# Seven products for eight in the first layer's last 1024 tokens, and second-layer weights in half-row portions

## Chip, cores, metric

One Trainium2 chip, one core. The metric is the device time of one execution in microseconds (us); lower is better.

## What is computed

Sliding-window attention, then two feed-forward layers on the same 2304 tokens, all in float32:

```python
scores = scale * np.matmul(q, k.transpose(0, 1, 3, 2))      # 4 x 8 heads x 576 x 64
scores = np.where((rel >= 0) & (rel < 64), scores, -1e9)
attn = softmax(scores); x = attn @ v                        # x: 2304 x 512
h = x @ w_in1;  g = np.maximum(h, 0.0) ** 2;  x = g @ w_out1    # 512 -> 2048 -> 512
h = x @ w_in2;  g = np.where(h > 0, h, np.exp(np.minimum(h, 0)) - 1);  out = g @ w_out2
```

The four weight matrices come as 64-bit floats and are turned into 32-bit values on the chip ("decode").

## The kernel before

The 2304 tokens are five blocks, `BLOCKS = [512, 256, 512, 512, 512]`, t = 0 to 4. The first layer's 2048 middle features are 16 groups of 128, j = 0 to 15. Every float32 operand is kept as a pair, a rounded high part and the rest as a low part (`split`, L105: ScalarE copies the high part, L107, and VectorE subtracts, L108), and every product is three matmuls: high by high, high by low, low by high (`mm3`, L355).

The first layer walks over (t, j), L735. `m_h(t, j)`, L362, is the first product of one group: 12 matmuls into a bank `ph`, then on ScalarE relu (L376) and square (L377) into `g`, then the split into `gs`, of which there are three. `m_out(t, j)`, L381, is the second product: 12 matmuls that add `gs` times the group's output weights to four banks `o`. First products run two groups ahead (LA = 2). After group 15 the block's result goes to DRAM (`x2d`). While block t is worked on, the attention of block t + 1 is done by pairs of heads p = 0 to 3 (a "unit"): `u_S` (scores, softmax: L276 on TensorE, L284 and L305 on VectorE, L289 on ScalarE), `u_T` (transposes, L317), `u_PV` (L330), `u_X` (split of the result into `xs`).

In block 0 the weights of the first layer are decoded (`w_split`, L152, with `decode64`, L135: one absolute value on ScalarE, then clamp, shift, and two merges on VectorE), each unit of `UNITS` one output group and the input group two further on.

The second layer's weights are prepared meanwhile. `make(i, p)`, L172, takes rows p and p + 8 of one matrix, decodes each row as a whole, forms the seven combinations that seven products need, splits each and writes it as a 256 KB piece (`wo`, L190) to DRAM. There are 16 such calls, at the places in `MAKE`, L433: two in block 1, four each in blocks 2 and 3, six in block 4. Their pieces pass through the four tiles `pt`, in block 4 through tiles of `xs`.

The second layer uses seven products of halves for eight already, in both products, on three stretches of 768 tokens (`step`, L596, `prod`, L564, `prod2`, L683). `x_make`, L506, forms the seven token operands, `unit_load`, L486, brings the prepared weights. Its order is written out by hand, by `in_turn`, L557, and a list.

The order on each engine inside the first layer is set by a scheduler that follows the program's order as a priority; the instructions of an engine then run in that order, each waiting for its semaphores. All loads and writes here are issued on one queue (SyncE, SP).

Of the kernel before, what the change touches and what calls it, by code (L numbers as in the profile page):

```python
# [25 lines left out]
def window_attention_then_two_mlps(  # L26
# [13 lines left out]
    nc = tc.nc  # L40
    HP, _, NT = k.shape
# [42 lines left out]
    def zeros():  # L84
        for x in qd:
            zero_q(x, nc.vector)
# [16 lines left out]
    last = {}  # L103

    def split(hi, lo, x, eng):  # L105

        last["hi"] = nc.scalar.activation(out=hi, in_=x, func=AF.Copy)  # L107
        last["lo"] = eng.tensor_tensor(out=lo, in0=x, in1=hi.bitcast(F32), op=ALU.subtract)  # L108

    def copy(out, in_, eng):  # L110
        if eng is nc.scalar:
            nc.scalar.activation(out=out, in_=in_, func=AF.Copy)
        else:
            eng.tensor_copy(out, in_)
# [8 lines left out]
    UNITS = [[(j, 0)] for j in range(LA)]  # L123
    UNITS += [[(j, 1)] + ([(j + LA, 0)] if j + LA < NJ else []) for j in range(NJ)]
    NU = len(UNITS)

    def w_load(u):

        m = len(UNITS[u])
        r = wts.tile([P, m, KD * P, 2], U32, tag=f"w{u}", name="wraw")  # L130
        for k, (j, i) in enumerate(UNITS[u]):
            nc.sync.dma_start(out=r[:, k].rearrange("p f w -> p (f w)"), in_=(w_in1, w_out1)[i][j])
        raw_w[u] = r

    def decode64(y, yf, lower, upper):  # L135

        nc.scalar.activation(out=yf, in_=upper.bitcast(F32), func=AF.Abs)  # L137
        nc.vector.tensor_scalar(  # L138
            out=yf, in0=yf, scalar1=SHORT, scalar2=TALL, op0=ALU.max, op1=ALU.min
        )  # L140
        nc.vector.tensor_scalar(
# [3 lines left out]
        nc.vector.scalar_tensor_tensor(  # L145
            out=y, in0=upper, scalar=0xC0000000, in1=y, op0=ALU.bitwise_and, op1=ALU.bitwise_or
        )
        nc.vector.scalar_tensor_tensor(
# [3 lines left out]
    def w_split(u):  # L152
# [5 lines left out]
        w = wts.tile([P, m, 2, KD * P], F32R, tag=f"w{u}", name="w")  # L158
        split(w[:, :, 0, :], w[:, :, 1, :], yf, nc.vector)
# [9 lines left out]
    wd1 = [drp.tile([P, 7, 2, HW], F32, name=f"wd1_{p}") for p in range(NP)]  # L169
    wd2 = {n: drp.tile([P, NP, 2, HW], F32, name=f"wd2_{n}") for n in ORD2}  # L170

    def make(i, p, big, small):  # L172

        y = big([P, 2, KD * P], "y")
        w = big([P, KD * P, 2], "praw")
        for r, j in enumerate((p, p + NP)):
            nc.sync.dma_start(out=w.rearrange("p f w -> p (f w)"), in_=(w_in2, w_out2)[i][j])
            decode64(y[:, r], y[:, r].bitcast(F32), w[:, :, 0], w[:, :, 1])
        y = y.bitcast(F32)
        q11, q12, q21, q22 = y[:, 0, :HW], y[:, 0, HW:], y[:, 1, :HW], y[:, 1, HW:]  # L180

        def put(k, x):
            o = small([P, 2, HW], "wo")
            if i:
                z = o.rearrange("p y (m a j) -> p y a m j", m=FT, j=TB)
                split(z[:, 0], z[:, 1], x.rearrange("p (a m j) -> p a m j", m=FT, j=TB), nc.vector)
            else:
                split(o[:, 0], o[:, 1], x, nc.vector)
            d = wd2[k][:, p] if i else wd1[p][:, ORD1.index(k)]
            nc.sync.dma_start(out=d, in_=o.bitcast(F32))  # L190

        def sub(x, a, b, op=ALU.subtract):
            nc.vector.tensor_tensor(out=x, in0=a, in1=b, op=op)

        if i:
            put(1, q11)
            put(2, q21)
            put(3, q22)
            sub(q12, q12, q11)
            put(5, q12)  # L200
            sub(q22, q22, q12)
            put(6, q22)
            sub(q11, q22, q11)
            put(7, q11)
            sub(q21, q21, q22)
            put(4, q21)
        else:
            put("a11", q11)
            put("a12", q12)
            put("a22", q22)  # L210
            sub(q21, q21, q22, ALU.add)
            put("s1", q21)
            sub(q11, q21, q11)
            put("s2", q11)
            sub(q12, q12, q11)
            put("s4", q12)
            sub(q22, q22, q11)
            put("s3", q22)

    raw = {}  # L220
# [3 lines left out]
    def u_load(u, parts="qkv"):  # L224
# [18 lines left out]
        if "k" in parts:  # L243
# [6 lines left out]
            if e:  # L250
                nc.vector.memset(kr[:, 0:WIN], 0.0)
# [14 lines left out]
    def u_S(u, alloc):  # L266
# [5 lines left out]
        for b0, m in banks(t):  # L272
# [9 lines left out]
            for i in range(m):  # L282
                c, b = slice(i * P, (i + 1) * P), b0 + i
                nc.vector.tensor_tensor_reduce(  # L284
# [4 lines left out]
                last["act"] = nc.scalar.activation(  # L289
# [4 lines left out]
            nc.vector.tensor_scalar(  # L294
                out=r, in0=sm[:, b0:b0 + m], scalar1=1.0e-9, scalar2=None, op0=ALU.add
            )
            nc.vector.reciprocal(out=r, in_=r)
            for i in range(m):
                c, b = slice(i * P, (i + 1) * P), b0 + i
                if t == 1:  # L300
                    nc.scalar.activation(
                        out=pb[:, c], in_=pb[:, c], func=AF.Copy, scale=rc[:, b:b + 1]
                    )
                    continue
                last["dve"] = nc.vector.tensor_scalar(  # L305
# [4 lines left out]
    def u_T(u, alloc):  # L310

        pts = []
        for b0, m in banks(u[0]):
# [5 lines left out]
            copy(pt[:, :m * P], ps[:, :m * P], nc.scalar)  # L319
# [16 lines left out]
    def u_X(u, ps):  # L336
        t, p = u
        n = BLOCKS[t]
        s = xs[t, p] = xp.tile([P, 2, NMAX], F32R, tag=f"xs{p}", name="xs")
        split(s[:, 0, :n], s[:, 1, :n], ps[:, :n], nc.vector)  # L340
# [21 lines left out]
    def m_h(t, j):  # L362
# [13 lines left out]
        nc.scalar.activation(out=g[:, :n], in_=ps[:, :n], func=AF.Relu)  # L376
        nc.scalar.activation(out=g[:, :n], in_=g[:, :n], func=AF.Square)  # L377
        split(s[:, 0, :n], s[:, 1, :n], g[:, :n], nc.vector)
        gs[t, j] = s

    def m_out(t, j):  # L381
# [12 lines left out]
        if j == NJ - 1:  # L394
            for m, ps in enumerate(acc[0]):
                e = e_tile(t)
                copy(e[:, :n], ps[:, :n], nc.vector if m % 2 else nc.scalar)
                nc.sync.dma_start(out=x2d[t][:, m, :], in_=e[:, :n])
# [33 lines left out]
    its = [(t, j) for t in range(NB) for j in range(NJ)]  # L432
    MAKE = {(1, 2), (1, 9)} | {(t, j) for t in (2, 3) for j in (1, 5, 9, 13)} | {(4, j) for j in (0, 1, 3, 4, 6, 7)}  # L433
    makes = [(i, p) for i in range(2) for p in range(NP)]
# [4 lines left out]
    CH = KD // 2  # L439
    la = []  # L440

    def e_tile(t):
        if la:
            return la[0].tile([P, 512], F32, tag="e4", name="ev", bufs=4)
        return at.tile([P, 512], F32, tag="pt", name="ev", bufs=4)

    turn = [0, 0]
    spare = []

    def big(shape, name):  # L450
        if name == "y" and la:
            turn[0] += 1
        if not la or turn[0] % 2:
            return wts.tile(shape, U32, tag="y", name=name, bufs=2)
        return wts.tile(shape, U32, tag="w0" if name == "y" else "w1", name=name)

    def small(shape, name):
        if la:
            if not spare:
                for k in range(KD):  # L460
                    x = xp.tile([P, 2, 2, HW], F32R, tag=f"xs{k}", name=name)
                    spare.extend((x[:, 0], x[:, 1]))
            turn[1] += 1
            return spare[turn[0] % 2 * KD + turn[1] % KD]
        return at.tile(shape, F32R, tag="pt", name=name, bufs=4)
# [3 lines left out]
    def gs_tile(name, n, m):  # L469
        k = g_turn[0] = (g_turn[0] + 1) % m  # L470
        if k < 4:
            return la[0].tile([P, 2, n], F32R, tag=f"gs{k}", name=name, bufs=1)
        return wts.tile([P, 2, n], F32R, tag=f"w{LA + NJ - 1}" if k == 4 else f"w{NJ - 1}", name=name)

    RING = [f"w{k}" for k in range(7, 15)]
# [30 lines left out]
    def x_make(b):  # L506
# [12 lines left out]
        b11, b12, b21, b22 = q[0, 0], q[0, 1], q[1, 0], q[1, 1]  # L519

        def put(i, x):
            if i < 5:
                o = wts.tile([P, 2, CH, NH], F32R, tag=f"w{LA + i}", name="xo")
            else:
                o = la[0].tile([P, 2, CH, NH], F32R, tag=f"xo{i}", name="xo", bufs=1)
            X[b, i] = o
            split(o[:, 0], o[:, 1], x, nc.vector)

        def sub(x, a, b):
            nc.vector.tensor_tensor(out=x, in0=a, in1=b, op=ALU.subtract)  # L530
# [3 lines left out]
        yield  # L534
        sub(b12, b12, b11)
# [28 lines left out]
    def prod(b, p, i, ps, first, final):  # L564
# [9 lines left out]

    tmp = {}
    rot2 = [0]

    def elu(h, x):
# [3 lines left out]
        nc.scalar.activation(out=r, in_=x, func=AF.Relu, scale=-1.0)  # L582
        last["act"] = nc.scalar.activation(out=r, in_=r, func=AF.Exp, scale=-1.0)
        last["dve"] = nc.vector.scalar_tensor_tensor(
# [5 lines left out]
    def add(out, a, b):  # L590
        nc.vector.tensor_tensor(out=out, in0=a, in1=b, op=ALU.add)  # L591

    def sub(out, a, b):
        nc.vector.tensor_tensor(out=out, in0=a, in1=b, op=ALU.subtract)

    def step(b, p, i):  # L596
# [4 lines left out]
        if i in (1, 6, 7):  # L601
            prod(b, p, i, q["x"], i == 1, False)
            nc.scalar.activation(out=tmp[i], in_=q["x"][:, :NH], func=AF.Copy)  # L603
# [27 lines left out]
    def g_split(b, k, p):  # L631
        if (b, k) == (NSB - 1, 4):
            if p % 2 == 0:
                room[0] = wts.tile([P, 2, 2, NH], F32R, tag=f"w{LA + p // 2}", name="g4")
# [4 lines left out]
        split(s[:, 0], s[:, 1], g[SRC[k]], nc.vector)  # L639
# [10 lines left out]
    def store(b, k, y, lo, hi, ms):  # L650
# [8 lines left out]
        for m in ms:  # L659
# [5 lines left out]
            nc.vector.transpose(out=o[:, :, m], in_=x.rearrange("p (b i) -> p b i", i=TB))  # L665
# [3 lines left out]
        def leave():  # L669
            for a in range(AB):  # L670
                c0 = dh * HW + a * FT * TB
                q_ = nc.scalar if n < NH and a % 2 else nc.sync
# [10 lines left out]
    def prod2(b, k, p, lo=0, hi=NH, ms=range(FT)):  # L683
# [20 lines left out]
        if k in (1, 6, 7):  # L704
            for m in range(FT):
                nc.scalar.activation(out=tmp[-k][:, m], in_=x[m][:, :NH], func=AF.Copy)
# [26 lines left out]
    for i in range(LA):  # L733
        m_h(*its[i])
    for i, (t, j) in enumerate(its):  # L735
# [146 lines left out]
```

## Time and profile before

| | |
|---|---|
| median of 3 runs | 840.34 us (840.02 to 842.02) |
| the profiled execution | 840.35 us, of which span 838.6 us |
| TensorE busy | 824.0 us |
| VectorE busy | 607.2 us |
| ScalarE busy | 546.3 us |
| moved by DMA | 185.48 MB |

The span runs from the first to the last instruction. Busy time is the time in which at least one instruction of the engine runs; TensorE's matmuls are pipelined and their ends modelled.

### The profile page before, as it was taken

How to read it: one execution, taken by the hardware profiler on the slowest of the kernel's cores; microseconds unless marked ns; L12 is line 12 of the kernel's file. 1: busy time of each engine (PE TensorE's matmuls, PEld its weight loads, DVE VectorE, ACT ScalarE, POOL GpSimd, SP SyncE). 2: the span in 40 equal slices, each digit the busy share in tenths (PEclk: the TensorE clock that was granted, in tenths of full speed). 3: DMA queues.
4: the chain of work that ended last, by engine and by line, in shares of the span. 5: the costliest groups of instructions: out<-in, count | busy, mean ns of one | idle time of the engine just before them, and what ended most of it. 6: DMA issues, size and time to landing. Idle time of an engine off the chain costs nothing.

```text
span 838.6 us, 14237 instructions
## 1 busy us (share of the span) xinstructions
PE 824.0 (98%) x4956; PEld 752.6 (90%) x4956; DVE 607.2 (72%) x1511; ACT 546.3 (65%) x1262; POOL 5.6 (1%) x21
## 2 busy tenths in 40 slices
PE   6899999999999999999999999999999999999998
PEld 5687879998888888888888899999999999999998
DVE  7999987675428575386696756698676799566875
ACT  6787867686447566575576667666477766477652
POOL 2000000000000000000000000000000000000000
PEclk9999999999999999999999999999999999999999
DMA  9991226455236563343869987878977876877832
GB/s 308 376 395 32 55 75 216 140 187 184 78 92 203 194 218 105 126 152 138 290 238 348 358 294 279 294 263 280 301 266 262 321 259 216 281 268 272 303 123 57
DMA packets 92807, 185.48 MB, mean 221 GB/s; under 512 B 43840, under 2 KB 50496, under 8 KB 84288
## 3 DMA queue, kind: packets, MB, share of 16 engines
q1 hardware_dynamic: 91904, 184.38, 64.6%
q8 instruction: 39, 0.64, 0.3%
q10 hardware_dynamic: 832, 0.20, 0.1%
q14 instruction: 32, 0.26, 0.1%
HBM read 145.75 MB, written 38.80 MB: 220 GB/s over the span
## 4 chain that ended last, share of the span: by engine, by line
PE 96%; DMA 1%; DVE 1%; ACT 1%; SPq 0%; issue 0%
PE ph L358 24%; PE o L358 24%; PE po L696 20%; PE px L569 8%; PE po L569 6%; PE py L569 6%; PE pa L276 3%; PE pa L330 2%; PE pa L317 2%; DMA wr<-wd 1%; PE px L696 1%; DVE pb L284 1%; DVE pb L305 1%; DMA qd<-in_q_dram 0%; PE po L276 0%; ACT pb L289 0%
## 5 line engine op out<-in xcount | busy, mean ns | idle before, releaser
L358 PE MATMUL ph<-xs,w 128*128 128x512 f32 (+1 forms) x960 | 220.8, 373 | 2.7 <-ACT xs L107 2.2
L358 PE MATMUL o<-gs,w 128*128 128x512 f32 (+1 forms) x960 | 216.3, 371 | 0.0
L358 PEld LDWEIGHTS ph<-xs,w 128*128 128x128 f32 x960 | 167.0, 189 | 33.1 <-ACT xs L107 3.1
L358 PEld LDWEIGHTS o<-gs,w 128*128 128x128 f32 x960 | 167.4, 188 | 29.6 <-DVE gs L108 0.2
L696 PE MATMUL po<-g,wr 128*128 128x384 f32 (+1 forms) x972 | 168.6, 333 | 0.0
L696 PEld LDWEIGHTS po<-g,wr 128*128 128x128 f32 x972 | 167.4, 188 | 0.0
L107 ACT ACTIVATE g<-gr 128x384 fp32r<-128x384 f32 x168 | 86.9, 524 | 55.5 <-PE po L696 49.6
L108 DVE TENSOR_TENSOR g<-gr,g 128x384 fp32r<-128x384 f32 x168 | 89.8, 550 | 16.1 <-ACT g L107 15.2
L569 PE MATMUL px<-xo,wr 128*128 128x384 f32 x432 | 83.8, 334 | 0.0
L108 DVE TENSOR_TENSOR gs<-g,gs 128x512 fp32r<-128x512 f32 (+1 forms) x80 | 50.6, 634 | 40.8 <-ACT gs L107 40.5
L569 PEld LDWEIGHTS px<-xo,wr 128*128 128x128 f32 x432 | 75.7, 188 | 0.2
L107 ACT ACTIVATE wo<-y 128x256 fp32r<-128x256 f32 x112 | 44.0, 411 | 47.9 <-DMA wd<-wo 20.3
L376 ACT ACTIVATE g<-ph 128x512 f32<-128x512 f32 (+1 forms) x80 | 43.6, 546 | 40.0 <-PE ph L358 39.0
L108 DVE TENSOR_TENSOR wo<-y,wo 128x256 fp32r<-128x256 f32 x112 | 45.5, 420 | 28.9 <-ACT wo L107 28.1
L289 ACT ACTIVATE pb<-pb,nm 128x128 f32<-128x128 f32 x144 | 55.9, 392 | 3.3 <-DVE nm L284 2.8
L138 DVE TENSOR_SCALAR y<-y 128x512 f32<-128x512 f32 (+1 forms) x50 | 24.8, 498 | 44.7 <-ACT y L137 44.3
L569 PE MATMUL po<-xo,wr 128*128 128x384 f32 x288 | 56.3, 334 | 0.3 <-DMA wr<-wd 0.3
L569 PE MATMUL py<-xo,wr 128*128 128x384 f32 x288 | 55.7, 334 | 0.0
L603 ACT ACTIVATE sy<-px 128x384 f32<-128x384 f32 x54 | 26.5, 491 | 38.0 <-PE px L569 38.0
L569 PEld LDWEIGHTS po<-xo,wr 128*128 128x128 f32 x288 | 50.4, 188 | 0.6 <-PE px L569 0.6
L569 PEld LDWEIGHTS py<-xo,wr 128*128 128x128 f32 x288 | 50.5, 188 | 0.1
L591 DVE TENSOR_TENSOR gr<-sy,py 128x384 f32<-128x384 f32 x48 | 26.6, 553 | 30.5 <-PE py L569 21.9
(74 smaller groups left out, 970.0 us busy)
## 6 DMA issues: line engine op xcount, KB each, us to landing
wr<-wd SPq DMA_DIRECT2D x66, 1024.0 KB, 5.9
wd<-wo SPq DMA_DIRECT2D x112, 256.0 KB, 4.0
wr<-wd SPq DMA_DIRECT2D x24, 768.0 KB, 4.8
wraw<-in_moe_w_in_dram SPq DMA_DIRECT2D x16, 512.0 KB, 9.8
vr<-in_v_dram SPq DMA_DIRECT2D x16, 512.0 KB, 5.7
wraw<-in_moe_w_out_dram SPq DMA_DIRECT2D x16, 512.0 KB, 9.7
praw<-in_moe_w_in_dram SPq DMA_DIRECT2D x16, 512.0 KB, 3.5
praw<-in_moe_w_out_dram SPq DMA_DIRECT2D x16, 512.0 KB, 3.8
```

Source lines behind the costliest of these rows:

```text
L107: last["hi"] = nc.scalar.activation(out=hi, in_=x, func=AF.Copy)
L108: last["lo"] = eng.tensor_tensor(out=lo, in0=x, in1=hi.bitcast(F32), op=ALU.subtract)
L138: nc.vector.tensor_scalar(out=yf, in0=yf, scalar1=SHORT, scalar2=TALL, op0=ALU.max, op1=ALU.min)
L276: nc.tensor.matmul(out=ps[:, i * P:(i + 1) * P], lhsT=qr[:, b0 + i].rearrange("p a x -> p (a x)"), rhs=kr[:, o:o + P], start=True, stop=True,)
L289: last["act"] = nc.scalar.activation(out=pb[:, c], in_=pb[:, c], func=AF.Exp, bias=nm[:, b:b + 1], scale=-1.0, accum_out=sm[:, b:b + 1],)
L317: nc.tensor.transpose(out=ps[:, i:i + P], in_=pb[:, i:i + P], identity=ident)
L358: last["pe"] = nc.tensor.matmul(out=ps, lhsT=a[x], rhs=b[y], start=(first and i == 0), stop=(final and i == 2))
L376: nc.scalar.activation(out=g[:, :n], in_=ps[:, :n], func=AF.Relu)
L569: last["pe"] = nc.tensor.matmul(out=ps[:, :NH], lhsT=w[:, wr_, c * P:(c + 1) * P], rhs=x[:, xr_, c], start=first and n == 0, stop=final an ...
L591: nc.vector.tensor_tensor(out=out, in0=a, in1=b, op=ALU.add)
L603: nc.scalar.activation(out=tmp[i], in_=q["x"][:, :NH], func=AF.Copy)
L696: last["pe"] = nc.tensor.matmul(out=ps[m][:, lo:hi], lhsT=w[:, y, m * P:(m + 1) * P], rhs=s[:, x, lo:hi], start=k in fresh and p == 0 and ...
```

## The change

**Blocks 3 and 4 together.** Their first products, 1024 tokens, are computed as seven products of halves. The 512 inputs are two halves, the 1024 tokens are the two blocks, and the 2048 features are eight pairs of groups (p, p + 8). A pair was 4 x 2 products of 128 x 128 by 512 for each half, and is now 7 x 2 (six matmuls for each of the seven). So `m_h` stays for blocks 0, 1 and 2 (TW = 2).

**Attention earlier.** The attention of blocks 3 and 4 is all done during block 2, one unit at each j; its result stays unsplit in `XQ`, and `x_make(-1)` forms the seven token operands `xo` (four combinations, seven splits of 128 x 1024).

**Weights of the seven products.** Three of the seven operands of a pair are the decoded weights themselves and are written to DRAM straight from `w` (24 writes). The four others are formed from high part plus low part, split and written (32 pieces, `put(2, ...)`). During the products each operand is loaded into one of ten tiles `ring` (`w0_load`, 56 loads of 256 KB).

**Half-row portions.** `make` is gone. `portions` is a list of small steps: for each weight pair four decodes of half a row (256 columns) and three groups of pieces. `slot(n)` takes the next n steps after the last VectorE and ScalarE instruction so far; `SLOTS` says where. Pieces pass through the unused upper halves of block 1's `xs`, then two halves of one tile (`tl`, rows below), from block 3 on also four tiles `wo`; the half rows come into four "lanes" (two of `praw`, two of `tl`).

**Block 0.** Units are now two output groups, then two input groups, and first and second products come in pairs.

```diff
+    for j in range(2, NJ, 2):
+        UNITS += [[(j + r, i) for r in range(2)] for j, i in ((j, 1), (j + LA, 0)) if j < NJ]
...
+    def portions():
+        y = lane["y"] = wts.tile([P, 2, KD * P], U32, tag="y", name="y", bufs=2)
...
+        for p in range(NP):
+            for r, j in enumerate((p, p + NP)):
+                w = wt[j, 0].bitcast(F32)
+                vec.tensor_tensor(out=yf[:, r], in0=w[:, 0], in1=w[:, 1], op=ALU.add)
+            for k, j, h in (("a11", p, 0), ("a12", p, 1), ("a22", p + NP, 1)):
+                nc.sync.dma_start(
+                    out=wd0[p][:, ORD1.index(k)], in_=wt[j, 0].bitcast(F32)[:, :, h * HW:(h + 1) * HW]
+                )
+            yield
+            sub2(q21, q21, q22, ALU.add)
+            put(2, p, "s1", q21)
...
+        for n, (i, p) in enumerate(TASKS):
+            for r in range(2):
+                for h in range(2):
+                    c = slice(h * HW, (h + 1) * HW)
+                    x = lanes.pop(0)
+                    decode64(y[:, r, c], yf[:, r, c], x[:, :, 0], x[:, :, 1])
+                    fetch(x)
+                    yield
...
-    MAKE = {(1, 2), (1, 9)} | {(t, j) for t in (2, 3) for j in (1, 5, 9, 13)} | {(4, j) for j in (0, 1, 3, 4, 6, 7)}
+    its = [(t, j) for t in range(TW + 1) for j in range(NJ)]
+    SLOTS = {(0, 14): 1, (0, 15): 1}
+    SLOTS |= {(1, j): 2 for j in range(NJ)}
+    SLOTS |= {(2, j): 5 if j < 9 else 3 for j in range(NJ)}
...
     def small(shape, name):
+        turn[1] += 1
         if la:
...
+        if lw and turn[1] % 6 < 4:
+            return lw[0].tile(shape, F32R, tag="wo", name=name, bufs=4)
+        if hw:
+            return half(2 + turn[1] % 2)
+        return xs[1, turn[1] % KD][:, :, HW:]
...
+    def stepw(p, i):
...
+        in_turn(prod, -1, p, i, q[k], i in (1, 2, 5), i in (4, 2, 3), NMAX)
+        w0_load()
+        q["done"].add(i)
+        if i in (1, 6, 7):
+            act.activation(out=tl[i], in_=q["x"], func=AF.Copy)
+        if i == 2:
+            f = sc.tile([P, NMAX], F32, tag="g", name="g")
+            add(f, tl[1], q["z"])
+            square(f)
+            ready(p, f)
...
+    for p in range(1, NP):
+        stepw(p, 1)
+        slot()
+        stepw(p, 2)
+        slot()
+        if p > 1:
+            in_turn(outw, p - 2 + NP)
+            slot()
+        stepw(p - 1, 3)
+        slot()
+        stepw(p, 6)
+        slot()
+        stepw(p - 1, 4)
+        in_turn(outw, p - 1)
+        slot()
+        if p < NP - 1:
+            stepw(p, 5)
+            slot()
+            stepw(p, 7)
```

(`outw(j)` is `m_out` for a `gs` that `ready` has split; block 3's 16 second products stand between the seven products, block 4's behind them.)

How the order moves. TensorE in block 0, before, then now (`ph` first product, `o_6..` the four banks of the second, `pa` attention); before, the first product of a group stands between parts of second products:

```order
L358 MATMUL ph<-xs,w 128x512 x10
L358 MATMUL o_666<-gs,w 128x512
L358 MATMUL o_667<-gs,w 128x512
L358 MATMUL o_668<-gs,w 128x512
L358 MATMUL o_669<-gs,w 128x512
L358 MATMUL ph<-xs,w 128x512 x2
```

```order
L467 MATMUL ph<-xs,w 128x512 x24
L420 MATMUL pa<-ident,pb 128x128
L433 MATMUL pa<-pt,vr 64x64 x8
L420 MATMUL pa<-ident,pb 128x128 x3
L467 MATMUL o_654<-gs,w 128x512
L467 MATMUL o_655<-gs,w 128x512
L467 MATMUL o_656<-gs,w 128x512
L467 MATMUL o_657<-gs,w 128x512
```

Now two first products (24) stand together and the second product of the first of them follows.

ScalarE in block 2, before, then now: the high parts of pieces (`wo` before, `tl` now) among relu and square (`g`) and the exponentials (`pb`):

```order
L107 ACTIVATE wo_2513<-y_2499 128x256
L107 ACTIVATE wo_2517<-y_2499 128x256
L107 ACTIVATE wo_2521<-y_2499 128x256
L107 ACTIVATE wo_2526<-y_2499 128x256
L376 ACTIVATE g_2397<-ph_2384 128x512
L377 ACTIVATE g_2397<-g_2397 128x512
L107 ACTIVATE wo_2531<-y_2499 128x256
```

```order
L53 ACTIVATE g_3662<-ph_3649 128x512
L53 ACTIVATE pb_3140,sm_3133<-pb_3140,nm_3132 128x128 x2
L53 ACTIVATE tl_2645<-y_1376 128x256
L53 ACTIVATE y_1376<-praw_2327 128x256
L53 ACTIVATE g_3662<-g_3662 128x512
L53 ACTIVATE pb_3160,sm_3133<-pb_3160,nm_3132 128x128 x4
L53 ACTIVATE y_1376<-tl_2644 128x256
L53 ACTIVATE gs_3663<-g_3662 128x512
L53 ACTIVATE tl_2645<-y_1376 128x256
L53 ACTIVATE pt_3248<-pa_3243 128x512
L53 ACTIVATE tl_2645<-y_1376 128x256
```

All pieces of this stretch now go through one tile, `tl_2645` (its two halves in turn), one or two at a time between the block's own work.

VectorE in the stage of the seven products, now (`gb`, `g` the sums from two products, `gs` the low part for a second product, `y` the portions, `wo` and `tl` low parts of pieces):

```order
L53 TENSOR_TENSOR gs_4676<-g_4673,gs_4676 128x512
L53 TENSOR_TENSOR tl_2645<-y_1376,tl_2645 128x4x2x32
L53 TENSOR_SCALAR y_1376<-y_1376 128x256 x5
L53 SCALAR_TENSOR_TENSOR y_1376<-tl_2644,y_1376 128x256 x2
L53 TENSOR_SCALAR y_1376<-y_1376 128x256
L53 SCALAR_TENSOR_TENSOR y_1376<-tl_2644,y_1376 128x256
L53 TENSOR_TENSOR gb_4728<-tl_4104,py_4701 128x512
L53 SCALAR_TENSOR_TENSOR y_1376<-tl_2644,y_1376 128x256
L53 TENSOR_SCALAR y_1376<-y_1376 128x256
L53 SCALAR_TENSOR_TENSOR y_1376<-praw_2327,y_1376 128x256
L53 TENSOR_TENSOR wo_4081<-y_1376,wo_4081 128x4x2x32
```

Portions stand between nearly all of the stage's own passes, where before block 4 had six whole calls of `make` up to group 7.

## Rows read from the trace of the kernel before

**Rows 1.** The page: busy time and share of the span; the core's span.
```profile
PE 824.0 (98%) x4956; PEld 752.6 (90%) x4956; DVE 607.2 (72%) x1511; ACT 546.3 (65%) x1262; POOL 5.6 (1%) x21
...
core 0: 838.6 us, clock 0.997
```

**Rows 2.** Busy time by stage: block 0, block 1, blocks 2 and 3, block 4.
```profile
core 0: us, PE busy (x) PEld busy (x) DVE busy (x) ACT busy (x) POOL busy (x), PEclk, DMA share, GB/s
42.00:136.00 94.00, 94.00 (x503) 77.39 (x502) 82.86 (x142) 70.08 (x137) 0.00 (x0) 1.00 0.40 136
136.00:200.00 64.00, 64.00 (x603) 62.15 (x602) 42.15 (x174) 45.61 (x147) 0.00 (x0) 1.00 0.57 183
200.00:404.00 204.00, 204.00 (x1214) 171.87 (x1213) 124.15 (x418) 124.93 (x324) 0.00 (x0) 1.00 0.46 152
404.00:488.00 84.00, 84.00 (x377) 70.22 (x376) 64.99 (x136) 52.44 (x106) 0.00 (x0) 1.00 0.89 315
```

**Rows 3.** Chain of waits: start, us, engine, tile, line, count.
```profile
138.59 1.44 PE ph L358 x12
...
210.28 2.72 PE ph L358 x12
...
218.44 1.78 PE pa L276 x16
...
242.01 2.02 PE pa L330 x64
```

**Rows 4.** TensorE's waits: us in total, times, longest.
```profile
PE ph L358 <- ACT xs L107: 2.2, 1, 2.2
```

**Rows 5.** ScalarE's groups: busy us, mean ns of one, idle before them.
```profile
L376 ACT ACTIVATE g<-ph 128x512 f32<-128x512 f32 x64 | 37.6, 590 | 37.7 <-PE ph L358 36.8 <-DVE gs L108 0.7
...
L377 ACT ACTIVATE g<-g 128x512 f32<-128x512 f32 x64 | 40.1, 629 | 1.2
...
L107 ACT ACTIVATE wo<-y 128x256 fp32r<-128x256 f32 x112 | 44.0, 411 | 47.9 <-DMA wd<-wo 20.3 <-DVE y L148 7.5 <-PE pa L330 6.2
...
L289 ACT ACTIVATE pb<-pb,nm 128x128 f32<-128x128 f32 x144 | 55.9, 392 | 3.3 <-DVE nm L284 2.8
...
L107 ACT ACTIVATE w<-y 128x1024 fp32r<-128x1024 f32 x14 | 14.8, 1057 | 0.1
```

**Rows 6.** VectorE's groups, same columns; the first and the last of 46 included.
```profile
L108 DVE TENSOR_TENSOR g<-gr,g 128x384 fp32r<-128x384 f32 x168 | 89.8, 550 | 16.1 <-ACT g L107 15.2
...
L108 DVE TENSOR_TENSOR gs<-g,gs 128x512 fp32r<-128x512 f32 x64 | 43.9, 687 | 36.6 <-ACT gs L107 36.3
...
L193 DVE TENSOR_TENSOR y<-y 128x256 f32<-128x256 f32 x64 | 26.0, 420 | 0.6
...
L108 DVE TENSOR_TENSOR w<-y,w 128x1024 fp32r<-128x1024 f32 x14 | 17.1, 1219 | 1.1 <-ACT w L107 1.1
...
L138 DVE TENSOR_SCALAR y<-y 128x512 f32<-128x512 f32 x36 | 15.2, 425 | 42.5 <-ACT y L137 42.4
...
L138 DVE TENSOR_SCALAR y<-y 128x1024 f32<-128x1024 f32 x14 | 9.6, 687 | 2.1 <-ACT y L137 1.9
...
L251 DVE MEMSET kr<- 128x64 f32 x4 | 0.3, 112 | 0.1
```

**Rows 7.** VectorE's passes in order of time; then its best stretch, and 20 to 120 us.
```profile
367.53 0.68 DVE L108 TENSOR_TENSOR gs<-g,gs 128x512 fp32r<-128x512 f32 x1
368.14 0.68 DVE L148 SCALAR_TENSOR_TENSOR y<-praw,y 128x512 uint32<-128x512 uint32 x1
...
40.00:60.00 20.00, 20.00 (x99) 16.73 (x98) 19.87 (x39) 16.93 (x33) 0.00 (x0) 1.00 1.01 389
...
sum 100.00, PE 96.89 PEld 76.64 DVE 93.45 ACT 80.08 POOL 0.00; mean PE 19.38 PEld 15.33 DVE 18.69 ACT 16.02 POOL 0.00
```

**Rows 8.** Pieces: ScalarE in front of one, the square behind it, all landing times.
```profile
291.20 0.42 ACT L107 ACTIVATE wo<-y 128x256 fp32r<-128x256 f32 x1 [4.19 <-DMA wd<-wo]
291.52 0.62 ACT L377 ACTIVATE g<-g 128x512 f32<-128x512 f32 x1
...
DMA to landing us min/median/max: 2.0/4.0/8.3
```

More of the change, by code (lines that the diff above doesn't have):

```diff
@@ L220, in window_attention_then_two_mlps, with slot @@
+    todo = portions()
+    count = [0]
+    def slot(n=1):
+        for _ in range(n):
+            with tc.issue_after(last["cd"].ins), tc.issue_after(last["ca"].ins):
+                quiet.append(1)
+                if next(todo, 0) is None:
+                    count[0] += 1
+                quiet.pop()
+    CH = KD // 2
+    TW = NB - 3
+    XQ = {}
     raw = {}
@@ L470, in gs_tile @@
         k = g_turn[0] = (g_turn[0] + 1) % m
[L471 to L475, printed above, removed]
+        return la[0].tile([P, 2, n], F32R, tag=f"gs{k}", name=name, bufs=1)
+    RING = [f"out{k}" for k in range(NP)]
     units = []
@@ L745, in window_attention_then_two_mlps @@
                 u_V2([(t + 1, p - 1), u], a_alloc)
-        if t == NB - 1 and j == NJ - 3:
+        else:
+            if j == 7:
+                att.close()
+                lw.append(pool(lwx, "lw", 1))
+                w0_load(10)
+            if j == 4:
+                xw = x_make(-1, NMAX)
+                next(xw)
+            if j in (8, 9):
+                next(xw)
+            if j == 14:
+                tl.update({k: lw[0].tile([P, NMAX], F32, tag=f"tl{k}", name="tl") for k in (1, 6, 7)})
+            if j > 13:
+                stepw(0, j - 13)
+        if t:
+            m_out(t, j)
+        if t == 0:
+            decode(min(LA + 3 + j, NU))
+        slot(SLOTS.get((t, j), 0))
+    for i in (6, 5, 7):
+        stepw(0, i)
+        slot()
+    for p in range(1, NP):
+        stepw(p, 1)
[14 more added lines that the diff above has]
+            stepw(p, 5)
+            slot()
+            stepw(p, 7)
+        else:
+            stepw(p, 7)
+            in_turn(outw, p - 1 + NP)
+            slot()
+            stepw(p, 4)
+            stepw(p, 5)
+            in_turn(outw, p)
+            slot()
+            stepw(p, 3)
+            in_turn(outw, p + NP)
+    leave1(TW + 1)
+    lwx.close()
+    la.append(pool(ctx, "la", 1))
+    xm0 = x_make(0)
+    for j in range(NJ + 2):
+        if j < NJ:
+            ready(j, rest[j % NP][:, j // NP])
+        j -= 2
+        if j < 0:
+            continue
+        if j in (1, 4, 7):
+            next(xm0)
+        if j < 12:
+            slot(1)
+        if j in (4, 8, 12):
+            unit_load()
+        if j == NJ - 3:
             sy = [wts.tile([P, 2, NH], F32, tag="y", name="sy", bufs=2) for _ in range(2)]
```

377 lines of the change are left out of this document (247 added, 130 removed).

## The prediction

> **What bounds the kernel now.** The core's span is 838.6 us [rows 1]; the profiled execution took 840.35 us, so 1.75 us lie outside the span, and it stands 0.01 us from the median of the three runs, 840.34. I read the busy table first: TensorE is busy for 98% of the span, VectorE for 72%, ScalarE for 65% [rows 1]. A busy TensorE need not be a full one, so the second view is the table by stage: from block 0 to the second layer TensorE is busy without a gap (94.00 of 94.00 us, 204.00 of 204.00) at a granted clock of 1.00 [rows 2]. Third, the chain of waits in steady state: twelve 512-column matmuls of one product take 2.72 us, over and over; the small ones between them are known too [rows 3]. So one 512-column matmul costs 2.72 / 12 = 0.227 us. Fourth, TensorE's waits: the longest after the start is one of 2.2 us [rows 4]. TensorE bounds the kernel; what leaves its list is gained in full, as long as VectorE and ScalarE keep handing over in time.
>
> **What the change removes.** Of the first layer's matmuls only the first product of blocks 3 and 4 changes. Before, these are 2 blocks x 16 x 12 = 384 matmuls of 512 columns; now 8 groups x 7 products x 6 = 336. The rest of TensorE's list keeps its counts. 48 x 0.227 = **10.9 us** less. If everything else hides, the profiled time is 840.35 - 10.9 = 829.4 us.
>
> **Block 0.** The same decodes and matmuls stand in another order: two first products, then two second products. The first excerpt of the order shows 24 `ph` matmuls in a row, then `o`. The g of the first of the pair now has 10 to 12 matmuls (2.3 to 2.7 us) to become ready; its chain of relu, square, high part and low part is 0.590 + 0.629 + 0.63 + 0.687 = 2.54 us [rows 5, 6], the high part being a copy of the square's size. Only its last step, the low part, is missing at 1.85 us, and the first four `o` matmuls (0.9 us) do without it. VectorE is busy for 82.86 of 94.00 us here [rows 2], mostly with decodes of 1.2 us [rows 6] that can stand in front. Bounds: nothing, and half of one such pass (0.6 us) in each of 7 pairs, 4 us. I take 1 us, near the lower end, since TensorE loses nothing in this stage now with the same VectorE load.
>
> **Block 2.** It now holds the attention of two blocks. One 512-token attention unit costs TensorE 1.78 (scores) + 8 transposes at the same 0.111 = 0.89, and half of a 2.02 us row = 1.01, together 3.7 us [rows 3]. That is moved work, not new. Between the last g of block 1 and the last g of block 2 TensorE has 192 + 156 matmuls of 512 columns, 33 of 256 columns (1.44 / 12 = 0.12) and some 7.6 units: 79.0 + 4.0 + 28 = 111 us. ScalarE's list for that stretch holds 64 exponentials at 0.392, 60 quarter-size passes (256 columns) at 0.41, 67 passes at 0.59 to 0.63 and 3 of 1.06 [rows 5]: 25 + 24 + 41 + 3 = 93 us. VectorE's list there is 106 us, worked out as in the next stage (117 us of durations x 0.905). Both fit under 111, at 84% and 95%.
>
> What is new is the staging. Of the pieces (256 KB, hi and lo) that go to DRAM here, 28 alternate between two halves of one tile; before there were four tiles (second excerpt). A round trip of one half is 0.42 (hi) + 0.42 (lo) + 0.5 (issue) + 4.0 (landing, median) = 5.3 us [rows 5, 6, 8], so 28 pieces need 14 x 5.3 = 75 us of the 111. On average that hides; where pieces stand close it shows as ScalarE waits, and behind such a wait stand the relu and square of the next g: in the trace of before ScalarE sat 4.19 us in front of a piece and the square behind it came only then [rows 8]. TensorE forgives that now, since g is used two products later. The cost lies between 0 (today's 20.3 us of such waits [rows 5] cost TensorE nothing) and the case of the first rival; I take 1 us with the hand-over to the seven products, where the last combinations (1.2 us each on VectorE) are due 27 + 12 + 3 = 42 matmuls, 9.5 us, after the last attention product and take 0.69 + 5 x 1.219 + 5 x 0.42 = 8.9 us [rows 6].
>
> **The stage of the seven products (blocks 3 and 4).** TensorE: from the last g of block 2 to the last g that the products hand over, 36 + 324 + 168 = 528 matmuls, 120 us. ScalarE: 103 passes at about 0.41, 103 at about 0.61 and 4 of 1.06, 109 us. VectorE: 72 + 105 quarter-size three-operand passes at 0.42, 72 shifts and clamps of 256 columns (0.29, an estimate: 0.425 at 512 and 0.687 at 1024 give 0.51 ns a column), 42 passes of 512 at 0.687 and 7 of 1024 at 1.219: 74 + 21 + 29 + 9 = 133 us of durations [rows 6]. Passes overlap: two neighbours that don't need each other start 0.61 us apart at a duration of 0.68 [rows 7]. Over the whole kernel the durations of VectorE's 46 groups add up to 671 us (first and last in [rows 6]) and its busy time is 607.2 [rows 1], a ratio of 0.905; 133 x 0.905 = **120 us, as much as TensorE has**. So this stage runs with VectorE full. Bounds: nothing, if it is as well packed as the best stretch of before, 19.87 of 20.00 us; and 120 / 0.935 - 120 = 8 us, if it packs only as from 20 to 120 us (93.45 of 100 us) [rows 7]. TensorE waits only when VectorE falls behind by more than the slack, which is some products. I take the middle, **4 us**: the list is full of passes that wait for ScalarE or a landing.
>
> **DMA and SyncE.** Added are 24 direct writes of high and low parts, 32 written pieces and 56 loads of one operand each: 112 x 256 KB = 29 MB; the decode loads come as 64 halves for 32. Blocks 1 to 4 move 64 x 183 + 204 x 152 + 84 x 315 = 69 MB in 352 us [rows 2]; with 23 MB more (the 24 direct writes fall mostly in block 0) in 341 us that is 270 GB/s. The rows give 183 / 0.57 = 321 to 315 / 0.89 = 354 GB/s at a full share, so it fits, at a share of 0.76 to 0.84. I cost it at nothing beyond the landing times above. Second layer: same lists, nothing.
>
> **Sum.** -10.9 + 1 + 1 + 4 = -4.9: 840.35 - 4.9 = **835.4 us**.
>
> **Rivals.**
> All of it hides: VectorE stays as dense as in its best row, and 829 to 832 us come out. For it: TensorE lost nothing in block 0 at a busy VectorE [rows 2, 4]. Against it: VectorE had 12% to spare there, here none. 0.20.
> The gain is eaten: the waits of the three places reach their upper ends, 4 + 1 + 8 = 13, or most of it: 838 to 843 us. 0.18.
> Slower, by the staging in block 2: with two halves ScalarE is bound by landings once 14 round trips exceed 111 us, a round trip of 7.9 us, that is a landing of 6.6 us. The median was 4.0, the longest 8.3 [rows 8], when loads of v stood in the queue; here eight such units load in the same stretch. At 8.3 us the round trip is 9.6, 14 x 9.6 = 134, 23 us more: 840.35 - 10.9 + 23 + 4 = 856; at 7.5 us, 14 x 8.8 = 123, 12 us more, 845. For it: pieces of 256 KB among other loads. Against it: at most two pieces are now in flight, where up to six were. 0.15.
> Slower, by the DMA engines themselves: if these many 256 KB transfers sustain less than 270 GB/s, blocks 1 to 4 wait for data; at 255 GB/s, 92 MB take 361 us for 341, and with the 4.9 us less of the sum the time is 855. No row of before shows so low a rate at a full share. 0.04. The Trainium skill (DMA: Bandwidth & Descriptors, section Bandwidth) speaks for this rival: it asks for transfers of at least 1 MiB for 75% of the peak and lists 138 GB/s for 64 KB and 341 for 1 MB. By that rule the transfers would bound blocks 1 to 4 and the change would lose: at 240 GB/s, an estimate from the middle of that page's two figures, the bytes above take 383 us; the rows of before, with their own 256 KB pieces at 315 GB/s in block 4, do not bear it out so far.
>
> **How the numbers follow.** The forecast's own band, 832 to 838, has 0.42; the remaining 0.01 goes to slower for what I have not seen. Changes under 0.3% (2.5 us) can't be told from none here, so faster means below 837.8 and slower above 842.9. Faster: 0.42 + 0.20 = 0.62; same 0.18; slower 0.20. The range leaves out little below 829 and the worse half of the slower cases: 829 to 846.
>
> **What would show it.** Right: 336 matmuls of 512 columns on a new line for the seven products and 48 fewer in all; TensorE's gaps between the hand-over from block 2 and the end of the products, 2 to 8 us in sum, released by ScalarE's copies or VectorE's g; VectorE at 19 or more of 20 us there; the second layer of the same length within 1 us. Wrong: long ScalarE waits for written pieces in block 2 with TensorE gaps behind them (first slower rival); a DMA share near 1.0 there (second); no TensorE gap at all (829); or gaps in block 0 of more than 4 us.

## The result and the profile after

The changed kernel takes 829.9 us (median of 4 runs, 828.8 to 830.28), the kernel before, on the same chip, 840.18: a ratio of 0.9872, 95% interval 0.9854 to 0.9891, or 10.3 us less. The forecast was 835.4, 4.9 us less. The sign and the cause were right, but nearly all of the 10.9 us of the removed matmuls came out, where the forecast took 6 us of waits off them.

The page after, busy time and share of the span [rows 1]:

```profile
span 828.5 us, 14865 instructions
...
PE 813.0 (98%) x4908; PEld 743.3 (90%) x4908; DVE 666.4 (80%) x1747; ACT 571.8 (69%) x1353; POOL 5.8 (1%) x21
```

TensorE has 48 matmuls fewer (4956 to 4908) and 11.0 us less busy time (824.0 to 813.0): its list became shorter by what was worked out, and still fills 98% of a shorter span. All else grew: VectorE by 59 us, ScalarE by 25. TensorE's groups, count | busy us, mean ns | idle before them, show the 192 + 144 = 336 matmuls of the seven products:

```profile
L685 PE MATMUL px<-xo,w 128*128 128x512 f32 x192 | 46.6, 390 | 0.7 <-ACT tl L53 0.7
L685 PE MATMUL py<-xo,w 128*128 128x512 f32 x144 | 36.5, 390 | 0.0
```

Then the table by stage [rows 2]: block 0, block 2 and the 120 us of the seven products (columns: window, length, busy time of PE, PEld, DVE, ACT, POOL with counts, granted clock, DMA share, GB/s).

```profile
42.00:136.00 94.00, 93.63 (x509) 77.41 (x509) 84.43 (x185) 72.10 (x158) 0.00 (x0) 1.00 0.59 202
...
191.00:302.00 111.00, 111.00 (x792) 94.76 (x792) 93.40 (x397) 84.66 (x257) 0.00 (x0) 1.00 0.67 212
...
302.00:422.00 120.00, 119.27 (x554) 98.39 (x549) 108.37 (x288) 91.06 (x203) 0.00 (x0) 1.00 0.98 348
```

The three places that were priced at 1, 1 and 4 us lost 0.37 us (block 0), 0.73 us (the start of the stage) and nothing else. TensorE's waits name them [rows 4]:

```profile
PE px L685 <- ACT tl L53: 0.7, 1, 0.7
...
PE ph L467 <- ACT w L53: 0.3, 1, 0.3
```

VectorE was busy for 108.4 of 120 us, not 120. The DMA engines were at a share of 0.98 in these 120 us; the 0.76 to 0.84 that were foreseen are an average over blocks 1 to 4, and there (136 to 477 us) it is 0.79. The end of the first layer shows where there is room. First SyncE's list (start, us, issue), then TensorE's:

```profile
443.17 0.43 SPq L240 DMA_DIRECT2D wd<-wo  x1
...
447.54 3.95 SPq L629 DMA_DIRECT2D xq<-x2d  x6
```

```profile
427.92 38.26 PE L467 MATMUL o<-gs,w 128*128 128x512 f32 x168
466.02 1.23 PE L685 MATMUL px<-xo,wr 128*128 128x384 f32 x6
```

The last product of blocks 3 and 4 ends before 428, but pieces (`wd<-wo`) go on until 443: weight work is also done beside block 4's second products, where the program places the last of its portions. Behind the last piece go the loads of the second layer's first activations (`xq`, 447.5), from which its operands `xo` are made; TensorE asks for them at 466.0 and does not wait. From there the second layer takes 828.5 - 466.0 = 362.5 us; before, its first product started at 475.64, which leaves 363.0. All the gain is in the first layer.

### The profile page after: what moved, and what is told of

It reads as the page before. It is cut to its first block, busy times and chain, and to the rows that moved or that the text cites. A ratio compares the mean times of both kernels' runs of the same rounds, so it can differ in the third digit from the quotient of the medians.

```text
span 828.5 us, 14865 instructions
## 1 busy us (share of the span) xinstructions
PE 813.0 (98%) x4908; PEld 743.3 (90%) x4908; DVE 666.4 (80%) x1747; ACT 571.8 (69%) x1353; POOL 5.8 (1%) x21
## 4 chain that ended last, share of the span: by engine, by line
PE 90%; DMA 6%; SPq 2%; ACT 2%; issue 0%; DVE 0%; ACTq 0%
PE o L467 22%; PE po L883 20%; PE px L685 14%; PE ph L467 12%; PE py L685 10%; PE po L685 6%; PE pa L379 3%; DMA wraw<-in_moe_w_out_dram 2%; PE pa L433 2%; PE pa L420 1%; DMA wd<-w 1%; PE px L883 1%; DMA wraw<-in_moe_w_in_dram 1%; DMA qd<-in_q_dram 1%; DMA wd<-tl 1%; SPq L342 0%
## 5 line engine op out<-in xcount | busy, mean ns | idle before, releaser
L467 PE MATMUL ph<-xs,w 128*128 128x512 f32 (+1 forms) x576 | 126.8, 361 | 2.8 <-ACT xs L53 2.2
L467 PEld LDWEIGHTS ph<-xs,w 128*128 128x128 f32 x576 | 94.9, 190 | 17.9 <-ACT xs L53 2.7
L53 DVE TENSOR_TENSOR g<-gr,g 128x384 fp32r<-128x384 f32 x168 | 90.0, 552 | 16.1 <-ACT g L53 15.1
L53 ACT ACTIVATE sy<-px 128x384 f32<-128x384 f32 x69 | 33.8, 490 | 42.5 <-PE px L685 42.0
L53 DVE TENSOR_SCALAR y<-y 128x256 uint32<-128x256 uint32 (+4 forms) x162 | 55.7, 366 | 6.8 <-ACT y L53 6.2
L53 DVE TENSOR_TENSOR gr<-gr 128x384 f32<-128x384 f32 x96 | 52.2, 553 | 0.5
L53 DVE TENSOR_TENSOR gs<-g,gs 128x512 fp32r<-128x512 f32 (+1 forms) x64 | 39.7, 621 | 11.7 <-ACT gs L53 11.2
L685 PE MATMUL px<-xo,w 128*128 128x512 f32 x192 | 46.6, 390 | 0.7 <-ACT tl L53 0.7
L685 PEld LDWEIGHTS px<-xo,w 128*128 128x128 f32 x192 | 36.0, 188 | 8.6 <-ACT tl L53 1.2
```

Source lines behind the costliest of these rows:

```text
L53: r = fn(*a, **kw)
L467: last["pe"] = nc.tensor.matmul(out=ps, lhsT=a[x], rhs=b[y], start=(first and i == 0), stop=(final and i == 2))
L685: last["pe"] = nc.tensor.matmul(out=ps[:, :NH], lhsT=w[:, wr_, c * P:(c + 1) * P], rhs=x[:, xr_, c], start=first and n == 0, stop=final an ...
```

## The experiments

The theories, as the expectations name them. A: TensorE's list alone sets the time. B, the prediction's reckoning: VectorE's list holds TensorE back in the stage of the seven products. C: the DMA engines are next. D, formed after the first four runs: pieces may slide, and all they have to meet is one deadline, the `xq` loads at the layer boundary. S: the round trip of a staging half binds. Times below are medians beside 829.9 of the change; ratios are against the kernel before, measured beside the run. The scheduler sets the lists anew around each edit, so a microsecond or so may come from there; that was not measured apart.

**Six products.**

```
-        in_turn(prod, -1, p, i, q[k], i in (1, 2, 5), i in (4, 2, 3), NMAX)
+        if i != 7:
+            in_turn(prod, -1, p, i, q[k], i in (1, 2, 5), i in (4, 2, 3), NMAX)
```

> Leaves out the matmuls of product 7 of every group in blocks 3 and 4 (8 x 6 = 48 matmuls of 512 columns, 10.9 us of TensorE), all else kept; the output is not the reference's. Theory A (room left: VectorE's list of the seven-product stage is worth the 108.4 us that it was busy there between 302 and 422 us, so TensorE alone sets the time): 829.9 - 10.9 = 819.0, at most 821, with VectorE at 19.5 or more of 20 us. Theory B (the prediction's reckoning: VectorE's list takes as long as TensorE's there, and only the queue's depth hid it): 828 to 830, nothing gained. Theory C (the DMA engines, 0.98 busy over the same 120 us, are next): 0.98 x 120 = 117.6 us of transfers, so 2 to 3 us gained, 827, with a DMA share of 1.0 and TensorE waiting for the loaded parts of the weights.

831.11 us, ratio 0.9905 (0.9886 to 0.9924): nothing gained. The time is near B's, the place is not. TensorE's list in order of time, with its waits of over 0.2 us in brackets:

```profile
413.92 1.52 PE L685 MATMUL py<-xo,w 128*128 128x512 f32 x6
415.28 38.50 PE L467 MATMUL o<-gs,w 128*128 128x512 f32 x168
458.69 0.69 PE L685 MATMUL px<-xo,wr 128*128 128x384 f32 x1 [4.91 <-ACT xo L53]
```

Behind the hand-over the stage ran without a wait of over 0.2 us and was over at 415 instead of 428, so neither VectorE nor the DMA engines held the products. The gain was lost at the boundary: `xq` was issued at 451.47, 3.9 us later than with seven products, 4.91 us of waiting follow (6.7 with the three behind it), and then the matmuls start at the lower clock: the first takes 0.69 us, where 0.334 is usual, and the granted clock is 0.78 from 460 to 480 (the number before the DMA share):

```profile
460.00:480.00 20.00, 18.56 (x74) 15.76 (x74) 12.40 (x17) 10.04 (x17) 0.00 (x0) 0.78 0.43 138
```

The sum: TensorE is at the boundary 12.2 us earlier, waits 4.9 there, and the second layer takes 827.4 - 458.7 = 368.7 us for 362.5, 1.8 of them in the other three waits and some 4.4 by the lower clock. That leaves 1.1 us of span.

**Eight products.**

```
         in_turn(prod, -1, p, i, q[k], i in (1, 2, 5), i in (4, 2, 3), NMAX)
+        if i == 7:
+            in_turn(prod, -1, p, i, q[k], i in (1, 2, 5), i in (4, 2, 3), NMAX)
```

> Issues the matmuls of product 7 twice (its sum is added twice, so the output is not the reference's): 48 more matmuls of 512 columns, so TensorE's list has as many as before the change, with all other work of the change kept. Theory A: 829.9 + 10.9 = 840.8, within 1 us of the kernel before; all that the change adds beside TensorE's list then costs 0 to 1 us. Theory B: VectorE was holding TensorE back and is given time: less than the 10.9, 834 to 838. Theory C: as B, 838 or less.

841.23 us, ratio 1.002 (1.001 to 1.003). 48 matmuls cost 11.3 us between the medians, or 12.0 when each kernel is taken against the one before beside it; 10.9 were worked out, and 1.1 more are a longer wait at the hand-over (`px<-xo` for `tl`, 1.8 us for 0.7). With them back the kernel stands 0.2% above the one before: all that the change adds beside TensorE's list costs 1 to 2 us, a little more than A's 0 to 1.

**More VectorE work in the pieces**, 24 passes and 70 passes (shown is the edit with 70; with 24 the condition also has `turn[1] % 6 >= 4`, the pieces on the two halves):

```
         o = small([P, 2, HW], "wo")
+        again = 1 if lw and not la else 0
...
             split(o[:, 0], o[:, 1], x, vec)
+            for _ in range(again):
+                vec.tensor_tensor(out=o[:, 1], in0=x, in1=o[:, 0].bitcast(F32), op=ALU.subtract)
```

> In the seven-product stage 24 low-part passes of 256 columns of the written pieces (those on the two halves) are done a second time, 24 x 0.42 = 10 us of VectorE more, with the same output. Theory A: 108.4 + 10 = 118.4 of the 119.3 us of TensorE: 830 to 832. Theory B: the list is full already, so all of it shows: 838 to 840. Theory C: no more bytes, no change: 830.

> As before, but all written pieces of that stage, 70 passes, 70 x 0.42 = 29 us more of VectorE. Theory A: 108.4 + 29 = 137.8 us against 119.3 of TensorE: 18 us over, so 829.9 + 18 = 848, less what slides behind the stage, 843 to 849. Theory B: all of it, 857 to 859. Theory C: as A.

830.74 us (0.9899, 0.9874 to 0.9924) and 845.99 us (1.0077, 1.0061 to 1.0093). The times are A's; its picture of a stage that fills up is not. VectorE from 302 to 422, with 24 and with 70 passes more:

```profile
302.00:422.00 120.00, 119.43 (x526) 98.24 (x525) 110.59 (x301) 91.19 (x201) 0.00 (x0) 1.00 0.97 339
```

```profile
302.00:422.00 120.00, 118.80 (x565) 97.66 (x561) 112.31 (x301) 88.08 (x191) 0.00 (x0) 1.00 0.92 318
```

It rose by only 2.2 and 3.9 us, and both times VectorE took in 13 passes more (x301 for x288); the rest of the work slid behind the stage. With 24 passes `xq` went at 451.48 and TensorE did not wait; with 70 at 469.74:

```profile
469.74 3.26 SPq L636 DMA_DIRECT2D xq<-x2d  x6
```

```profile
476.04 0.69 PE L692 MATMUL px<-xo,wr 128*128 128x384 f32 x1 [8.53 <-ACT xo L53]
```

When TensorE waits here, its first product starts 6.3 us behind `xq` (476.04 - 469.74; 7.2 with six products). In the changed kernel it starts 18.5 us behind, so the pieces have 11 to 12 us to spare. 22.2 us later less 12 leaves 10; the four waits at the boundary add up to 10.1. The second layer takes 368.1 us for 362.5, 1.6 of them waits, so about 4 of the other 6 come from the lower clock (0.78, then 0.88 in two stretches of 20 us). This is where D comes from.

**D by itself: `xq` earlier, and fewer decodes.** `xq` ahead of the second layer's first weights, with six products and with seven:

```
-                    nc.sync.dma_start(
+                    last["xq"] = nc.sync.dma_start(
...
         if j in (4, 8, 12):
-            unit_load()
+            with tc.issue_after(last["xq"].ins):
+                unit_load()
```

> Six products as in the first run (the matmuls of product 7 left out, output not the reference's), and the loads of the second layer's first activations (xq) stand in SyncE's list right behind the last written piece, ahead of the second layer's first weights; before, six weight loads stood ahead of them that wait for TensorE. Theory D (with six products the products' stage itself is 12 us shorter, and what it gains is given back at the layer boundary, where TensorE waited 6.7 us for xo): xq is issued at 447.6 instead of 451.5, the waits at the boundary shrink from 6.7 to 3 us, 826 to 828 for 831.1. Theory C (the DMA engines are full up to there, so that the order changes nothing): 830 to 832. Theory B (VectorE): as C.

> The changed kernel with seven products, with the xq loads right behind the last written piece and ahead of the second layer's first weights. Theory D: TensorE did not wait at the boundary, so nothing changes: 829 to 831. If the weights, now issued behind xq, land late: up to 834.

824.91 us with six (0.9811, 0.9797 to 0.9826): some 6 us of the 10.9 come back from an order of loads alone, more than expected, for two reasons. The waits at the boundary shrink from 6.7 to 2.9 us, and the granted clock, 0.78 from 460 to 480 before, now stays at 1.00. What TensorE waits for now is the weights (`px<-wr`, 2.9 us). 829.33 us with seven (0.9883, 0.9866 to 0.9900): no change, since nothing waited there.

The last two weight tasks written without load and decode, with seven products and with six:

```
-    HALVES = [(i, p, r, h) for i, p in TASKS for r in range(2) for h in range(2)]
+    HALVES = [(i, p, r, h) for i, p in TASKS[:14] for r in range(2) for h in range(2)]
...
-                    x = lanes.pop(0)
-                    decode64(y[:, r, c], yf[:, r, c], x[:, :, 0], x[:, :, 1])
-                    fetch(x)
+                    if n < 14:
+                        x = lanes.pop(0)
+                        decode64(y[:, r, c], yf[:, r, c], x[:, :, 0], x[:, :, 1])
+                        fetch(x)
```

> The changed kernel with seven products, but the last 2 of the second layer's 16 weight tasks are written without being loaded and decoded (8 half rows, 2 MB of loads, some 9 us of VectorE; the second layer then works with wrong weights there). Theory D (TensorE's list sets the time as long as the written pieces end by about 447 us; their end is a deadline with some 9 us to spare): the pieces end some 9 us earlier and nothing changes, 829 to 831. Theory B (VectorE holds TensorE back in the stage): faster, 822 to 826.

> Six products (the matmuls of product 7 left out) and the same 8 half rows not loaded or decoded. Theory D: the pieces end by some 438 us and xq can go before TensorE needs it, so that the 10.9 us that were lost at the layer boundary come out: 819 to 821, with less than 1.5 us of waits for xo. Theory B or C (the seven-product stage itself was bound): 826 or more.

With seven 829.97 us (0.9886, 0.9868 to 0.9904): the last piece goes at 430 instead of 443, and not a microsecond comes of it. With six 819.78 us (0.9771, 0.9746 to 0.9796): the last piece goes at 438.93, `xq` at 441.05, one wait of 0.5 us is left at the boundary, and the 10.9 us that had come to nothing come out: 829.97 - 819.78 = 10.2 us between the two. The pair separates the theories: an earlier end of the pieces gains nothing while TensorE reaches the boundary after `xo` is made, and all of it once TensorE would get there first.

**More VectorE work that can't slide.**

```
         split(s[:, 0], s[:, 1], f, vec)
+        if not la:
+            for _ in range(2):
+                vec.tensor_tensor(out=s[:, 1], in0=f, in1=s[:, 0].bitcast(F32), op=ALU.subtract)
```

> The low part of each of the 16 g of the seven-product stage is made three times, same output: 32 passes of 512 columns more on VectorE, 32 x 0.69 = 22 us, this time in the chain that TensorE waits for, where it can't slide. Theory D: the g go first and the written pieces slide; TensorE waits less than 2 us inside the stage, the pieces end some 11 to 22 us later and TensorE waits at the layer boundary: 836 to 842. Theory B (a full VectorE stalls the products): the waits stand inside the stage, between 309 and 440 us, 10 us or more, 840 to 845.

839.39 us (0.9995, 0.9985 to 1.0004). The time is D's; the place is B's, with half of its 10 us of waits. The pieces end at 454, 11 us later, but TensorE comes later too: its first product of the second layer starts at 474.66, 18.5 us behind `xq` (456.19) as in the change, and does not wait. It waits for `gs` towards the end of the stage:

```profile
PE o L467 <- DVE gs L53: 4.8, 3, 2.7
```

5.2 us with a wait for ScalarE's half of `gs`; the clock is at 0.83 from 422 to 442, and the second layer takes its 362.4 us. So VectorE can stall the products, as the prediction said, but here it took 22 us more of it in their own chain, and 9.5 us came of them.

**The DMA engines and the staging.** 24 pieces written twice, and one half for two:

```
+    wdx = drp.tile([P, 2, HW], F32, name="wdx")
...
         nc.sync.dma_start(out=d, in_=o.bitcast(F32))
+        if lw and not la and turn[1] % 6 >= 4:
+            nc.sync.dma_start(out=wdx, in_=o.bitcast(F32))
```

> 24 of the written pieces of the seven-product stage (those on the two halves) are written a second time to a spare place: 24 x 256 KB = 6.3 MB, 18 us of all DMA engines at the 348 GB/s of 302 to 422 us. Theory C (the engines are full there, 0.98): the pieces end 18 us later, of which 9 us are free until the boundary: 829.9 + 9 = 839, with TensorE waiting at the first product of the second layer. Theory A (TensorE alone): 829 to 831, the share staying near 1.0 for longer.

```
-            return half(2 + turn[1] % 2)
+            return half(2)
```

> The written pieces that alternated between two halves of one tile all use one half, so each waits for the landing of the one before. Theory S (the prediction's first slower rival, made worse by half the staging): a round trip of 5.3 us and 28 pieces make 148 us against the 111 of TensorE in block 2: 829.9 + 37 = 867, with ScalarE waiting for written pieces and TensorE for g behind it. Theory A (ScalarE has room and pieces can slide): up to 10 us, 830 to 840, the loss standing at the layer boundary and not in block 2.

851.78 us (1.0135, 1.0120 to 1.0151) and 878.49 us (1.0450, 1.0432 to 1.0467). Both lose most of it at the boundary and not where the pieces are made. Their waits at the first product of the second layer:

```profile
PE px L688 <- ACT xo L53: 13.9, 1, 13.9
```

```profile
PE px L685 <- ACT xo L53: 34.4, 1, 34.4
```

With one half the last pieces go at 500.20 and 502.60 and the first of `xq` between them at 500.57, 53 us later; ScalarE waits 56.7 us for landings of `wd<-tl`. TensorE still has 111.00 of 111.00 us in block 2, where 18 pieces now go out through `tl` instead of 28; the others slide. 53 less 12 is 41, and the four waits at the boundary are 38.9 us. So half the staging does bind, as the prediction's first slower rival had it, but TensorE pays at the layer boundary and not in block 2. In the other run the pieces end 31 us later for 6.3 MB, more than the 18 us that the engines need for them: ScalarE waited 19.5 us for a half to be free of its second write. Whether the engines' own rate would have bound was not separated from that.

**Block 0 in single steps.**

```
-        if t == 0 and j > 2 and j % 2:
-            m_out(t, j - 1)
-            m_out(t, j)
-        for n in ([i + LA] if t or j < 2 else [i + LA - 1, i + LA] if j % 2 else []):
+        for n in [i + LA]:
             if n < len(its):
                 m_h(*its[n])
-        if t == 0 and j < 2:
+        if t == 0:
             m_out(t, j)
```

> In block 0 TensorE does one first product and one second product in turn, as before the change, while the weights are still made two rows at a time. If the pairs cost TensorE the 1 us that the prediction priced: 829. If they cost nothing (0.3 us of waits in block 0): 830, and not faster; with rows made in twos and used one by one TensorE may wait for a decode, up to 834.

836.05 us (0.9943, 0.9926 to 0.9959), slower than all three numbers. Block 0 is the same (93.60 of 94.00 us). The loss is at the hand-over to the seven products: the first loads of their weights (`w<-wd`) stood in SyncE's list behind six pieces and four loads of half rows and were issued at 307.73, not 301.89. TensorE waited 2.0 us for them and 1.8 us for `xo`, and the granted clock was 0.91 from 310 to 330. The order of the pairs costs nothing in block 0; that hand-over is the second place where a load in SyncE's list is just in time.

## Why the prediction was right or wrong

- **TensorE bounds the kernel; what leaves its list is gained in full.** Right, and shown both ways (eight products 841.2, six with the boundary cleared 819.8). The 10.9 us measured 10.2 with six products and 11.3 to 12.0 with eight.
- **Block 0, +1 us.** 0.37 us.
- **Block 2 and hand-over, +1 us.** Block 2 nothing, the hand-over 0.73. Behind a landing (2.38 us in front of a piece, from 309.31 on without a break up to the copy) ScalarE came late to the first copy `tl<-px`: the mechanism that was named, at one place.
- **The stage of the seven products, +4 us.** This is the term that was mis-sized; beside the hand-over it measured 0. Two steps failed. The first is the price of VectorE's list, "133 x 0.905 = 120 us, as much as TensorE has". The list itself was right to the pass: from the last g of block 2 to the last low part that the products hand over stand 298 passes, with 132 us of durations (count times mean). They took 112 us, a ratio of 0.85:

```profile
302.99:426.58 123.59, 122.86 (x541) 101.24 (x542) 112.20 (x298) 94.42 (x211) 0.00 (x0) 1.00 0.97 344
```

The 671 us under the 0.905 are no sum of durations. They add up the groups' busy times, out of which the overlap inside each group is gone already: 64 passes of 420 ns are 26.9 us and stand with 26.0 [rows 6]. Count times mean over the 46 groups gives 695 us, a ratio of 0.874, and 133 x 0.874 = 116 us. The other 4 us come from the stage itself: there a pass loses 0.068 us to its neighbour on average ((132.4 - 112.2) / 298), in the whole kernel before 0.058, since more of them stand close behind one another (four in five overlap the next one there, three in four in the kernel before). With 112 us the prediction's own upper bound, 112 / 0.935 = 120 us, is no longer than TensorE's list, and nothing is left of the term. The same ratio priced VectorE's list of block 2 at 106 us; it was busy there for 93.4.

- **The second step of that term** is "TensorE waits only when VectorE falls behind by more than the slack, which is some products": the list was taken as due within its stage. But 249 of the 298 passes are portions, which nobody in the stage waits for. When there is more to do they slide: VectorE never passed 113 of 120 us there even with 29 us more, which is 0.94, the 0.935 of [rows 7], and the g of the products were served in between. The slack that counted was not some products but 11 to 12 us at the layer boundary, which the prediction never looked at. So a list of 120 us would not have cost the 4 us either: 24 passes (10 us) more cost nothing.
- **All of it hides, 829 to 832, at 0.20.** This is what happened. Against it stood "VectorE had 12% to spare there, here none"; it had 9%.
- **The slower rivals.** Neither came. Staging: the 28 pieces of block 2 landed in 2.6 us (median), not in 4.0 or the 6.6 at which the rival begins; ScalarE waited 8.6 us for them there and TensorE not at all. DMA: over blocks 1 to 4 the forecast of 270 GB/s at 0.76 to 0.84 held (268 at 0.79), but the average hid a stage at 0.98 and 348 GB/s, in which 21.5 MB of loads and pieces fall into 340 to 400 us alone. So the sign of this rival, a share near 1.0, was seen without its loss. The Trainium skill (DMA: Bandwidth & Descriptors, section Bandwidth) lists 138 GB/s for a transfer of 64 KB and 341 for one of 1 MB; the estimate of 240 from the middle of the two does not agree with the trace, which has 86 transfers of 256 KB in these 60 us at 5.2 us to landing, some seven under way at once (an estimate, 86 x 5.2 / 60), and moves up to 371 GB/s:

```profile
136.00:477.00 341.00, 340.26 (x2131) 293.51 (x2130) 287.80 (x918) 245.34 (x641) 0.00 (x0) 1.00 0.79 268
...
380.00:400.00 20.00, 20.00 (x90) 16.58 (x89) 19.00 (x55) 15.98 (x38) 0.00 (x0) 1.00 1.02 371
```

- **The second layer, same within 1 us.** 362.5 against 363.0.

Of the runs that compute the reference none beats the changed kernel: `xq` first is the same within the interval. Were TensorE's list cut again, the order of SyncE's list at the boundary would have to change with it.

## What to carry to other kernels

Before you price a full helper engine, sort its list: work that the bound engine waits for in the stage, and work that only has a deadline later. Price the second kind at its deadline (when is the last of it out, what is queued behind it, when does the bound engine ask?), not in the stage where it is issued. And where a cut gains nothing, look at the next place where the bound engine needs a load before you conclude that another engine was the limit: with six products 10.9 us vanished there, some 6 of them in a queue's order.

## What was not expected of the hardware

VectorE's passes overlap their successors by a fixed time, not a share. Passes in order of time in the changed kernel (start, us; x2 is two in a row):

```profile
305.75 0.42 DVE L53 TENSOR_TENSOR y<-y 128x256 f32<-128x256 f32 x1
306.08 1.22 DVE L53 TENSOR_TENSOR xo<-xr,xo 128x1024 fp32r<-128x1024 f32 x1
307.22 2.35 DVE L53 TENSOR_TENSOR xr<-xr 128x1024 f32<-128x1024 f32 x2
```

```profile
342.67 0.69 DVE L53 TENSOR_TENSOR gs<-g,gs 128x512 fp32r<-128x512 f32 x1
343.28 0.42 DVE L53 TENSOR_TENSOR y<-y 128x256 f32<-128x256 f32 x1
```

The next pass starts 0.33 us behind one of 0.42, 0.61 behind one of 0.69 and 1.14 behind one of 1.22: 0.08 to 0.09 us less each time. Over all pairs of this kernel that overlap, the medians by shape (with five pairs or more) are 0.076 to 0.093 us, from 128x1 to 128x1024. For passes of 256 columns that is a fifth, for 1024 columns a fifteenth; a list whose passes follow each other closely is priced by start-to-start times of its own shapes, with count times mean as the sum of durations.

A wait of some microseconds can cost TensorE more than its length: behind the 4.91 us with six products matmuls ran at half speed (0.69 for 0.334 us, the 1.2 GHz level), and of the 16.1 us that 70 passes cost, about 10 were waits and about 4 the lower clock. It need not: behind the 2.95 us with six products and `xq` first the granted clock stayed at 1.00.
